# One list that orders the loads, the q/k part and the first 21 steps of a fused attention and two-expert kernel

## The chip, the cores and the metric

The kernel runs on one core of a Trainium2 chip. The metric is the device time in microseconds of one execution; before the change the median of three runs is 1145.67 us.

## The reference

In short: the input tokens are 6016 rows of 256 channels. Attention runs over channels: q and k are normalised over the tokens, a 256 x 256 score matrix is formed, and a softmax over it mixes the channels of v. Two pairs of dense layers follow, each 256 to 2048 to 256, the first with a rational activation, the second with h * relu6(h + 3) / 6.

```python
qn = q / (np.linalg.norm(q, axis=1, keepdims=True) + 1e-06)
kn = k / (np.linalg.norm(k, axis=1, keepdims=True) + 1e-06)
s = kn.transpose(0, 2, 1) @ qn / tau
a = softmax(s)                    # rows of 256
x = (v @ a).reshape(6016, 256)
h = x @ w_in                      # float64 weights
g = (a0 + a1*h + a2*h*h + a3*h**3) / (1 + |b0|*|h| + |b1|*h*h + 1e-6)
x = g @ w_out
h = x @ w_in2
out = (h * clip(h + 3, 0, 6) / 6) @ w_out2
```

## The kernel before

**The front part.** q and k come in 14 chunks (QK_CHUNKS: 1, 2, ten of 4, 3 and 1 rows per partition). For each chunk ScalarE squares both tiles (L240), VectorE adds the squares into two accumulators (L242), and TensorE multiplies k against q (`products`, L250). When the accumulators are folded (L227), eight small matmuls sum them over the partitions (L281, L282), a chain of tiny VectorE and ScalarE instructions makes the inverse norms, a matmul with a diagonal matrix spreads the norms of q over the partitions (L304), ScalarE copies that row (L310), and the softmax follows (L319 to L327). The 256 x 256 result is then multiplied into w_in, in column groups W0a, W0b, W1, W2, W3 (L339), so that v goes straight into the first layer. ScalarE evicts the high half of each product (L349), VectorE the low half (L351); in the list these are E0ah0, E0al0 and so on.

**Weights.** The weights are float64 in memory. Each of the four matrices is loaded in four groups of 1 MB and made into a pair of tiles, high and low, by `conv`: piece s (ScalarE, L154), b (ScalarE, L156), j (VectorE, L160), h (ScalarE, L167) and the low half on VectorE (l) or POOL (p) (L171). `wi1:2b` is piece b of group 2 of the first w_in. w_in of the first expert needs only s, b and j.

**The steps.** v is cut into blocks of 384 and then eleven times 512 tokens. A step s handles two of the sixteen 128-row tiles of the hidden layer: M1 is the first layer of expert 1 (12 matmuls), then U1, P1 (ScalarE) and DS, P2, P3 (VectorE) read its PSUM tile h, and AB, LN, EX (ScalarE), HI, N2, DD (VectorE) and LO (VectorE) or LOP (POOL) make the high and low halves of the activation. M3 is the second layer for step s - 2. Ten steps behind, expert 2 runs: M2 (first layer), C1 (ScalarE), C2 (VectorE), H2 (ScalarE), L2 (VectorE) or L2P (POOL), M4. Yh and Yl split the output of expert 1 at the end of a block, Vh and Vl split v. In a full step TensorE does 48 matmuls of 512 columns.

**What sets the order.** TensorE, VectorE, ScalarE and POOL run in program order: `chain` ties each instruction to the one before on its engine. From the norm on, the program order up to step 21 is the list FILL, written out by hand; after it, and for what the list leaves out, the string ORDER repeats step by step. Loads go through SP's queue in the order in which they are called: q and k first (L233), then wi1, wo1, wi2 (L124, L127), with v and wo2 called where the list reaches certain steps. Buffers come from pools by tag (BUFS): three each of U, P, hi, lo, which hold the chunks of q and k first, two of B, C and st. A load into a buffer waits until its last readers are done. Instructions of two engines that read the same PSUM tile are put one after the other in program order. `shares` marks a VectorE instruction that reads two SBUF operands, and `behind` makes a POOL instruction wait for the last marked one.

Of the kernel before, what the change touches and what calls it, by code (L numbers as in the profile page):

```python
# [61 lines left out]
def attention_rational_relu6_kernel(ctx: ExitStack, tc, q, k, vT, tau, w_in, w_out, ca, cb, w_in2, w_out2, outT):  # L62
# [44 lines left out]

# [144 lines left out]

    for i in range(LAST + 1):
        load_chunk(i)
        if i == LAST:
            for n in (512, 256):
                for a in (acc_k, acc_q):
                    fold(a, n)
        squares(i)
        if i <= NORM_AT:  # L260
            products(i)
    nc.sync.dma_start(out=TAU, in_=tau.partition_broadcast(128))
    load_w("wi1", 0)
    nc.sync.dma_start(out=col[:, 4:6], in_=cb.partition_broadcast(128))
    nc.sync.dma_start(out=col[:, 0:4], in_=ca.partition_broadcast(128))
    load_w("wi1", 1)
    load_v(0)
    load_w("wi1", 2)
    load_w("wi1", 3)
    for name in ("wo1", "wi2"):  # L270
        for g in range(4):
            load_w(name, g)
# [3 lines left out]
    nc.vector.reciprocal(out=rt, in_=TAU)
    s2k, s2q = tails
    for i in range(4):
        a, t = ((acc_k, s2k), (acc_q, s2q))[i // 2]
        h = slice((i % 2) * 128, (i % 2) * 128 + 128)  # L280
        nc.tensor.matmul(ssp[:, 0, i:i + 1], a[:, h], ones[:, 0:1], start=True, stop=False)  # L281
        nc.tensor.matmul(ssp[:, 0, i:i + 1], t[:, h], ones[:, 0:1], start=False, stop=True)  # L282
# [19 lines left out]
    nc.vector.tensor_scalar(out=inv[:, 0:2], in0=inv[:, 0:2], scalar1=rt, scalar2=-1.0, op0=ALU.mult, op1=ALU.mult)
    products(LAST - 1)
    nc.tensor.matmul(ssp[:, 1, 0:256], ones, diag, start=True, stop=True)  # L304
    products(LAST)
    for p in "sbj":
        conv("wi1", 1, p)
    split_v(0, "h")
    split_v(0, "l")
    nc.scalar.activation(out=qb, in_=ssp[:, 1, 0:256], func=AF.Copy)  # L310
    conv("wi1", 2, "s")
# [324 lines left out]
```

## Time and profile before

| | |
|---|---|
| median of the runs | 1145.67 us (1145.56 to 1145.82) |
| span of the profiled execution | 1141.5 us |
| its own time | not recorded apart; with the median it leaves 4.2 us around the span |
| TensorE busy | 1100.4 us (96%), 4870 matmuls |
| VectorE busy | 1009.6 us (88%) |
| ScalarE busy | 819.8 us (72%) |
| POOL busy | 251.6 us (22%) |
| loaded and stored | 42.2 MB, nearly all loads in the first 83 us |

The span runs from the first instruction to the last. Busy shares are averages over stages with different limits: q/k products first, then the ramp of expert 1 with the weight pieces, then the steps of both experts. A row of the trace counts matmuls as the hardware issues them: a chunk of four rows has 16 in the q/k part.

### The profile page before, as it was taken

To read this page: it belongs to the slowest core of one execution; us is meant where nothing else is said; L and a number is where in the kernel's file an instruction comes from. 1 tells how busy PE (TensorE), PEld (TensorE's weight loads), DVE (VectorE), ACT (ScalarE), POOL (GpSimd) and SP (SyncE) were. 2 spreads that over 40 slices of the span, in tenths; PEclk is the share of its full clock that TensorE was granted. 3 is DMA by queue.
4 is the path that set the end of the run, shared out by engine and by line. 5 is a ranking of instruction groups with operands and counts; after the bars stand their busy time and mean duration, and the time that the engine had idled before them with its cause. 6 is when DMAs were issued, how large, how long until landed. Compare 5 with 4: busy or idle time off the path is not lost.

```text
span 1141.5 us, 12312 instructions
## 1 busy us (share of the span) xinstructions
PE 1100.4 (96%) x4870; PEld 914.1 (80%) x4870; DVE 1009.6 (88%) x872; ACT 819.8 (72%) x802; POOL 251.6 (22%) x115
## 2 busy tenths in 40 slices
PE   8986689999999999999999999999999999999998
PEld 7756578877888888888888888888888888888887
DVE  6689999988999999998998998998998999999954
ACT  6798986776776777777677676786776776776643
POOL 0013335222221222212212222122122221221200
PEclk9998899999999999999999999999999999999999
DMA  9980000000010010010010010010010010000000
GB/s 358 369 327 1 19 1 1 15 19 1 1 37 1 1 38 1 1 37 1 1 37 1 1 38 1 1 37 1 1 37 1 1 37 1 1 19 1 1 19 18
DMA packets 17464, 42.20 MB, mean 37 GB/s; under 512 B 1536, under 2 KB 2560, under 8 KB 17408
## 3 DMA queue, kind: packets, MB, share of 16 engines
q1 hardware_dynamic: 17408, 41.43, 9.9%
q8 instruction: 38, 0.62, 0.2%
q14 instruction: 18, 0.15, 0.0%
HBM read 35.26 MB, written 6.16 MB: 36 GB/s over the span
## 4 chain that ended last, share of the span: by engine, by line
PE 86%; DVE 6%; ACT 4%; issue 2%; DMA 1%; POOL 0%; SPq 0%; POOLq 0%; DVEq 0%; ACTq 0%
PE h L374 41%; PE y L379 21%; PE o L379 20%; PE y L250 3%; DVE B L421 1%; ACT P L406 1%; DVE P L430 1%; DVE P L416 1%; ACT U L411 1%; DVE hi L544 1%; DVE P L556 1%; DMA lo<-in_q_dram 1%; DVE B L550 1%; ACT U L434 0%; DVE q L160 0%
## 5 line engine op out<-in xcount | busy, mean ns | idle before, releaser
L485 POOL TENSOR_TENSOR lo<-C,hi 128x1024 fp32r<-128x1024 f32 (+1 forms) x82 | 195.4, 2383 | 680.5 <-DVE lo L561 649.6
L411 ACT ACTIVATE U<-h,col 128x1024 f32<-128x1024 f32 (+1 forms) x96 | 105.7, 1101 | 180.2 <-PE h L374 179.6
L374 PE MATMUL h<-vh,w 128*128 128x512 f32 (+1 forms) x768 | 194.7, 397 | 20.0 <-DVE P L430 18.8
L379 PE MATMUL y<-hi,wo 128*128 128x512 f32 (+1 forms) x800 | 198.7, 385 | 0.4 <-DVE hi L544 0.4
L374 PEld LDWEIGHTS h<-vh,w 128*128 128x128 f32 x768 | 147.9, 195 | 52.7 <-issue 21.5
L374 PE MATMUL h<-yh,wi 128*128 128x512 f32 (+1 forms) x768 | 187.1, 385 | 3.0 <-DVE C L474 1.8
L379 PE MATMUL o<-hi,wo 128*128 128x512 f32 (+1 forms) x736 | 182.6, 384 | 0.0
L421 DVE SCALAR_TENSOR_TENSOR B<-U,aB,h 128x1024 f32<-128x1024 f32 (+1 forms) x96 | 120.6, 1256 | 61.8 <-ACT P L406 61.6
L379 PEld LDWEIGHTS y<-hi,wo 128*128 128x128 f32 x800 | 149.3, 188 | 29.2 <-DVE hi L544 0.7
L374 PEld LDWEIGHTS h<-yh,wi 128*128 128x128 f32 x768 | 143.2, 188 | 32.3 <-DVE C L474 3.2
L379 PEld LDWEIGHTS o<-hi,wo 128*128 128x128 f32 x736 | 137.6, 188 | 26.6
L469 ACT ACTIVATE C<-h,imm 128x1024 f32<-128x1024 f32 (+1 forms) x96 | 105.1, 1095 | 62.6 <-PE h L374 60.0
L474 DVE SCALAR_TENSOR_TENSOR C<-C,h 128x1024 f32<-128x1024 f32 (+1 forms) x96 | 114.0, 1187 | 16.1 <-ACT C L469 16.1
L544 DVE SCALAR_TENSOR_TENSOR hi<-P,col,U 128x1024 fp32r<-128x1024 f32 (+1 forms) x96 | 125.3, 1306 | 1.0 <-ACT U L438 0.9
L430 DVE SCALAR_TENSOR_TENSOR P<-P,col,h 128x1024 f32<-128x1024 f32 (+1 forms) x96 | 120.7, 1257 | 3.9 <-ACT U L411 1.2
L556 DVE SCALAR_TENSOR_TENSOR P<-P,col,B 128x1024 f32<-128x1024 f32 (+1 forms) x96 | 121.0, 1261 | 2.7
L406 ACT ACTIVATE P<-h,col 128x1024 f32<-128x1024 f32 (+1 forms) x96 | 113.3, 1181 | 6.9 <-PE h L374 5.1
L550 DVE SCALAR_TENSOR_TENSOR B<-B,hi 128x1024 f32<-128x1024 f32 (+1 forms) x96 | 115.8, 1207 | 2.7
L416 DVE TENSOR_TENSOR P<-P,h 128x1024 f32<-128x1024 f32 (+1 forms) x96 | 114.5, 1193 | 3.4 <-ACT U L411 1.9
L480 ACT ACTIVATE hi<-C 128x1024 fp32r<-128x1024 f32 (+1 forms) x96 | 99.6, 1037 | 23.8 <-DVE C L474 21.8
L379 PE MATMUL y<-lo,wo 128*128 128x512 f32 (+1 forms) x400 | 108.3, 388 | 7.6 <-POOL lo L561 7.6
L434 ACT ACTIVATE U<-B,imm 128x1024 f32<-128x1024 f32 (+1 forms) x96 | 108.9, 1134 | 2.7
(101 smaller groups left out, 1296.6 us busy)
## 6 DMA issues: line engine op xcount, KB each, us to landing
raw_wi<-in_moe_w_in_dram SPq DMA_DIRECT2D x8, 1024.0 KB, 13.4
raw_wo<-in_moe_w_out_dram SPq DMA_DIRECT2D x8, 1024.0 KB, 15.1
vo<-in_v_dram SPq DMA_DIRECT2D x11, 512.0 KB, 3.7
out_dram<-vo SPq DMA_DIRECT2D x10, 512.0 KB, 2.8
...
```

Source lines behind the costliest of these rows:

```text
L374: nc.tensor.matmul(h[j], w_in_at(name, a, c, f + j), x[b][:, c, :], start=(i == 0), stop=(i == 5))
L379: nc.tensor.matmul(y[d], w_out_at(name, a, 2 * pr + j, d), g[b][j], start=(pr == 0 and i == 0), stop=(pr == 7 and i == 5))
L406: nc.scalar.activation(out=halves(c["P"], T), in_=c["h"], func=AF.Identity, scale=A3, bias=A2)
L411: nc.scalar.activation(out=halves(c["U"], T), in_=c["h"], func=AF.Abs, scale=B1)
L416: nc.vector.tensor_tensor(out=p, in0=p, in1=c["h"], op=ALU.mult)
L421: nc.vector.scalar_tensor_tensor(out=halves(c["B"], T), in0=halves(c["U"], T), scalar=aB0, in1=c["h"], op0=ALU.add, op1=ALU.mult)
L430: nc.vector.scalar_tensor_tensor(out=p, in0=p, scalar=A1, in1=c["h"], op0=ALU.add, op1=ALU.mult)
L474: nc.vector.scalar_tensor_tensor(out=x, in0=x, scalar=6.0, in1=h, op0=ALU.min, op1=ALU.mult)
L485: i2 = e.tensor_tensor(out=x, in0=y, in1=z.bitcast(F32), op=ALU.subtract)
L544: shares(nc.vector.scalar_tensor_tensor(out=c["Hi"][:, fa], in0=P[:, fa], scalar=A0, in1=U[:, fa], op0=ALU.add, op1=ALU.mult))
L550: shares(nc.vector.scalar_tensor_tensor(out=B[:, fa], in0=B[:, fa], scalar=ONE_EPS, in1=c["Hi"][:, fa].bitcast(F32), op0=ALU.add, op1=ALU. ...
L556: shares(nc.vector.scalar_tensor_tensor(out=P[:, fa], in0=P[:, fa], scalar=A0, in1=B[:, fa], op0=ALU.add, op1=ALU.subtract))
```

## The change

The loads, the q/k part and the norm are cut into pieces with names of their own and put into FILL, which now begins the program. `lq3` loads chunk 3 of q, `lwi12` loads group 2 of the first w_in, `lst`, `lsa`, `lsb` the scalars, `lv1` block 1 of v; `sq3` squares, `aq3` adds, `x3` multiplies, `fk512` folds, `nT` to `nC` are the norm, `zm0` to `zr0` the softmax. ORDER is unchanged.

- Loads: q13 and k9 come early; the first weight load (wo1:0) comes between q10 and q11, more between and behind the last chunks; wo2 and v are called from the list.
- Weight pieces of wo1:0, wi1:0, wi1:2, wo1:1, wo1:2, wi2:2 stand between the pieces of the q/k part, the norm and the softmax.
- The norm matmuls (nM) come after product x11; before, after x10.
- The order of all steps to 21 is another, also the order in which U1, P1, DS, P2, P3 read a PSUM tile. LOP stands 18 times (14 before), LO 2 (6), L2P 8 (6), L2 3 (5); weight low halves are 8 on POOL and 4 on VectorE in both, but other ones.
- The tiles of the low halves (Lo, L2, vl, yl) are asked for where they are written, not with the high halves.
- LOP now waits for the last marked VectorE instruction (`behind`).

```diff
 FILL = (
...
+    "lq0 lk1 lk0 lk2 sq0 aq0 lq1 sq1 lq2 lq13 sq2 lk3 x0 sk0 x1 lq3 lq5 ak0 aq1 sq3 sk1 lk4 x2 lq4 aq2 ak1 lk9 sk2 lk5 lst x3 ak2 "
+    "sq4 x4 lq6 lq7 lsb aq3 sk3 aq4 ak3 x5 sq5 lk6 lq8 sk5 aq5 sk4 sq7 x6 sq6 ak4 ak5 lk8 aq6 lk7 sk6 ak6 sk8 lk10 x7 sk7 sq8 lq9 "
+    "aq7 ak7 lq10 ak8 sq9 aq8 sk9 x8 ak9 sk10 sq10 lwo10 lq11 lk11 aq9 lk13 lk12 lq12 aq10 wo1:0b x9 lwi10 wo1:0s ak10 wo1:0j sk11 "
+    "sq11 sq12 ak11 wo1:0h aq11 sk12 x10 aq12 sq13 ak12 fk512 x11 sk13 nB lwo11 fq512 fk256 wi1:0s wi1:0b wo1:1b nT wo1:1s fq256 "
+    "lwi12 lwo12 nM wi1:0j n0 wi1:2b wo1:0p n1 x12 lwi22 n2 wi1:2s wo1:2s nD x13 nC wo1:2b wi1:2j zm0 ze0 zm1 wi2:2s ze1 lwi11 zt0 "
+    "zc0 wi1:1s wi1:1b wi2:2b zt1 wo1:1j zc1 lv0 zr0 lwi13 wi1:1j W0a wo1:2j E0ah0 W0b Vh lwo13 wi2:2j E0ah1 E0al0 wi1:3s W1 wi1:3b "
+    "E0bh1 Vl E0al1 M1@0 E0bh0 E1h1 lsa wo1:2h E1h0 U1@0 lwi20 P1@0 E0bl1 wi1:3j E0bl0 M1@1 E1l1 wo1:1h lwo20 E1l0 U1@1 P2@0 W3 "
+    "DS@0 P1@1 wo1:1p P3@0 P2@1 DS@1 P3@1 AB@0 M1@2 LN@0 wo1:2p E3h1 EX@0 AB@1 E3l1 lv1 M1@3 E3h0 HI@1 E3l0 W2 N2@1 LN@1 EX@1 HI@2 "
+    "P1@2 U1@2 DD@1 N2@2 wo1:3s wi2:2h E2h0 LOP@1 P2@2 E2h1 DS@2 P3@2 AB@2 DD@2 U1@3 E2l1 LN@2 LOP@2 E2l0 M1@4 EX@2 DS@3 HI@3 "
+    "wo1:3b N2@3 wo1:3j P1@3 AB@3 P1@4 DD@3 U1@4 P2@3 LN@3 M3@2 DS@4 wi2:2p LOP@3 P2@4 wo2:0s lwi21 M3@3 P3@3 AB@4 M1@5 P3@4 EX@3 "
+    "LN@4 M1@6 EX@4 HI@4 U1@5 HI@5 wi2:0b N2@4 P1@5 N2@5 wo2:0b wi2:1s DD@4 P2@5 DS@5 LOP@4 M3@4 U1@6 P3@5 DD@5 wo2:0j AB@5 P1@6 "
+    "M1@7 P2@6 Vh@7 LN@5 LOP@5 DS@6 P3@6 EX@5 M3@5 HI@6 Vl@7 AB@6 LN@6 N2@6 EX@6 M1@8 HI@7 wo2:0h M3@6 lwo23 wo1:3h lwo22 P1@7 DD@6 "
+    "lwo21 N2@7 U1@7 wi2:0s LO@6 DD@7 P2@7 U1@8 M3@7 wo2:0p P1@8 wo2:2b DS@7 DS@8 P3@7 P2@8 AB@7 LOP@7 wo1:3p LN@7 M1@9 EX@7 AB@8 "
+    "LN@8 wo2:1s P3@8 M1@10 EX@8 HI@8 wi2:0j U1@9 N2@8 P1@9 lwi23 wi2:0h wi2:1b HI@9 DD@8 wo2:1b N2@9 LOP@8 M3@8 P1@10 U1@10 M3@9 "
+    "P2@9 DS@9 Yh@9 AB@9 LN@9 DD@9 P3@9 P2@10 Yl@9 wi2:0p EX@9 lv2 LOP@9 P3@10 DS@10 M2@10 wo2:2s M1@11 C1@10 HI@10 wi2:1j M3@10 "
+    "N2@10 wo2:2j AB@10 LN@10 DD@10 EX@10 U1@11 P1@11 C2@10 LOP@10 P2@11 DS@11 P3@11 H2@10 L2P@10 wi2:1h AB@11 HI@11 M3@11 M2@11 "
+    "C1@11 wo2:2h M1@12 wi2:1l C2@11 LN@11 H2@11 U1@12 wo2:2l M2@12 P1@12 C1@12 N2@11 DD@11 M4@11 DS@12 EX@11 AB@12 C2@12 L2P@11 "
+    "P2@12 LN@12 P3@12 LOP@11 EX@12 H2@12 M4@12 M2@13 HI@12 N2@12 C1@13 M1@13 wo2:1j U1@13 DD@12 M3@12 C2@13 P1@13 wi2:3b wo2:1h "
+    "P2@13 LOP@12 DS@13 L2P@12 M2@14 M3@13 P3@13 HI@13 AB@13 LN@13 wo2:1l wi2:3s N2@13 C1@14 M1@14 H2@13 wi2:3j M4@13 DD@13 U1@14 "
+    "C2@14 P1@14 L2P@13 P2@14 LOP@13 wi2:3h DS@14 P3@14 M4@14 M2@15 EX@13 HI@14 H2@14 N2@14 M1@15 M3@14 AB@14 wi2:3l DD@14 LN@14 "
+    "EX@14 C1@15 L2P@14 U1@15 C2@15 P1@15 Vh@15 P2@15 DS@15 LOP@14 AB@15 P3@15 LN@15 HI@15 M2@16 M4@15 M3@15 Vl@15 M1@16 N2@15 "
+    "EX@15 C1@16 wo2:3s HI@16 C2@16 U1@16 DD@15 N2@16 LO@15 P1@16 M2@17 DD@16 H2@15 P2@16 LOP@16 wo2:3b DS@16 P3@16 L2@15 M3@16 "
...
+    "AB@20 L2@19 HI@20 H2@20 N2@20 DD@20 LOP@20 P1@21 U1@21 C1@21 LN@20 DS@21 C2@21 M4@20 EX@20 P2@21 L2P@20 AB@21"
 )
...
+    def square(x, i):
+        s2 = sq[x, i] = wtile("B" if x == "k" else "st")[:, 0:QK_CHUNKS[i] * 256]
+        nc.scalar.activation(out=s2, in_=chunks[x, i], func=AF.Square)
...
             @add
             def HI():
                 first = pend.pop(a)
                 U, B, P = c["pend"] = first["U"], first["B"], first["P"]
-                c["Hi"], c["Lo"] = wtile("hi", F32R), wtile("lo", F32R)
+                c["Hi"] = wtile("hi", F32R)
...
             def lo(e):
                 U, B, P = c["pend"]
+                c["Lo"] = wtile("lo", F32R)
+                hl1[a] = [halves(c[t], Ta) for t in ("Hi", "Lo")]
                 i = e.tensor_tensor(out=c["Lo"][:, fa], in0=P[:, fa], in1=U[:, fa], op=ALU.mult)
-                if e is nc.vector:
-                    shares(i)
+                (shares if e is nc.vector else behind)(i)
...
-            if n == "M1" and int(at) % 8 == 4:
-                load_v(int(at) // 8 + 1)
+        elif n[0] == "l":
+            if n[1] in "kq":
+                load_chunk(n[1], int(n[2:]))
...
             w1_matmuls(n[1:])
-            if n != "W0a":
-                load_w("wo2", int(n[1]))
```

## Rows read from the trace of the kernel before

**Rows 1.** Busy by stretch: length, PE, PEld, DVE, ACT, POOL, clock, DMA, GB/s.
```profile
50.00:59.88 9.88, 7.45 (x30) 4.91 (x29) 6.82 (x13) 8.28 (x12) 0.00 (x0) 1.00 1.05 391
59.88:144.21 84.33, 59.10 (x246) 49.47 (x244) 76.88 (x80) 78.12 (x89) 24.52 (x11) 0.88 0.28 104
144.21:162.64 18.43, 15.46 (x73) 12.80 (x73) 18.16 (x17) 15.80 (x16) 9.01 (x4) 1.00 0.00 0
162.64:210.16 47.52, 46.69 (x228) 40.92 (x228) 44.67 (x41) 33.92 (x36) 16.44 (x6) 1.00 0.00 1
210.16:255.78 45.62, 44.90 (x204) 37.88 (x205) 41.56 (x34) 32.81 (x32) 11.19 (x6) 1.00 0.06 21
255.78:272.73 16.95, 14.43 (x61) 11.03 (x60) 12.84 (x12) 11.61 (x11) 4.58 (x2) 1.00 0.00 0
272.73:1128.00 855.27, 855.27 (x3775) 708.43 (x3774) 768.29 (x632) 601.27 (x564) 183.16 (x76) 1.00 0.04 12
```

**Rows 2.** Timeline of TensorE: start, us, line, operation, count [idle before, releaser].
```profile
37.48 3.62 PE L250 MATMUL y<-lo,hi 128*128 128x256 f32 x16
...
40.93 0.28 PE L281 MATMUL o<-ones,accs 128*128 128x1 f32 x2
...
48.76 0.59 PE L304 MATMUL o<-yl,ones 128*128 128x256 f32 x2
...
59.88 1.96 PE L374 MATMUL h<-vh,w 128*128 128x384 f32 x8
...
162.64 1.67 PE L374 MATMUL h<-yh,wi 128*128 128x384 f32 x8 [1.05 <-DVE C L474]
```

**Rows 3.** Waits of TensorE and VectorE, 60 to 165 us: total us, times, longest.
```profile
PE h L374 <- DVE P L430: 16.2, 5, 7.3
...
PE y L379 <- POOL lo L561: 7.4, 3, 4.2
...
DVE w L351 <- ACT w L349: 3.6, 3, 1.8
```

**Rows 4.** Busy time by stretch, two stretches of the q/k stage.
```profile
10.00:20.00 10.00, 10.00 (x48) 8.79 (x48) 9.00 (x9) 8.23 (x9) 0.00 (x0) 1.00 1.02 413
...
30.00:40.00 10.00, 10.00 (x48) 8.81 (x47) 9.56 (x12) 7.16 (x9) 0.00 (x0) 1.00 0.87 316
```

**Rows 5.** Timeline of ScalarE (two rows), then of VectorE (two rows), q/k stage.
```profile
9.72 1.06 ACT L240 ACTIVATE st<-lo 128x1024 f32<-128x1024 f32 x1 [0.80 <-DMA lo<-in_q_dram]
...
12.29 1.06 ACT L240 ACTIVATE st<-P 128x1024 f32<-128x1024 f32 x1 [0.22 <-DMA P<-in_q_dram]
...
21.04 1.23 DVE L242 TENSOR_TENSOR accs<-accs,st 128x1024 f32<-128x1024 f32 x1
...
37.75 1.96 DVE L227 TENSOR_TENSOR accs<-accs 128x512 f32<-128x512 f32 x4
```

**Rows 6.** Groups by line: count, busy us, mean ns, idle before.
```profile
L156 ACT ACTIVATE raw_wo<-raw_wo,imm 128x1024 int32<-128x1024 uint16 x8 | 10.0, 1247 | 0.0
```

**Rows 7.** Timeline of VectorE: an evict, a weight piece, the instruction after it.
```profile
67.96 0.75 DVE L351 SCALAR_TENSOR_TENSOR w<-o,small,w 128x512 fp32r<-128x512 f32 x1
...
91.26 1.22 DVE L160 SCALAR_TENSOR_TENSOR q<-q,raw_wo 128x1024 int32<-128x1024 int32 x1
...
92.39 1.01 DVE L556 SCALAR_TENSOR_TENSOR P<-P,col,B 128x768 f32<-128x768 f32 x1
```

**Rows 8.** Timeline of VectorE (two rows of line 544), then of POOL.
```profile
137.49 2.92 DVE L544 SCALAR_TENSOR_TENSOR hi<-P,col,U 128x1024 fp32r<-128x1024 f32 x1
...
143.78 1.27 DVE L544 SCALAR_TENSOR_TENSOR hi<-P,col,U 128x1024 fp32r<-128x1024 f32 x1
...
137.48 1.84 POOL L561 TENSOR_TENSOR lo<-P,U 128x768 fp32r<-128x768 f32 x1
```

**Rows 9.** Timeline of VectorE, then of TensorE, where the list ends.
```profile
266.02 1.28 DVE L421 SCALAR_TENSOR_TENSOR B<-U,aB,h 128x1024 f32<-128x1024 f32 x1 [2.78 <-ACT P L406]
...
269.89 2.09 PE L374 MATMUL h<-vh,w 128*128 128x512 f32 x8 [1.23 <-DVE P L430]
```

More of the change, by code (lines that the diff above doesn't have):

```diff
@@ L251, in products @@
                                  qt[:, r * 256:(r + 1) * 256], start=(first[i] + r == 0), stop=(first[i] + r == PER - 1))
[L253 to L272, printed above, removed]
-    rt = small[:, 0:1]
[L276 to L282, printed above, removed]
@@ L283, in attention_rational_relu6_kernel @@
-    for p in "sbj":
-        conv("wi1", 0, p)
-    products(NORM_AT + 1)
+        parts_done.append(i)
+    rt = small[:, 0:1]
     aB0 = const.tile([128, 1], F32, name="aB0")
-    nc.scalar.activation(out=aB0, in_=B0, func=AF.Abs)
     ss, ln, y0, iy, nrm, inv = (small[:, 4 * j:4 * j + 4] for j in range(1, 7))
-    nc.vector.tensor_scalar(out=ss, in0=ssp[:, 0, 0:4], scalar1=1e-30, scalar2=None, op0=ALU.max)
-    nc.scalar.activation(out=ln, in_=ss, func=AF.Ln)
-    nc.scalar.activation(out=y0, in_=ln, func=AF.Exp, scale=0.5)
@@ L302, in attention_rational_relu6_kernel @@
[L302 to L311, printed above, removed]
     nmax, sm, rs = small[:, 28:30], small[:, 30:32], small[:, 2:4]
-    ep = ptile("h1")
@@ L316, in attention_rational_relu6_kernel @@
-    eT = halves(wtile("hi"), 256)
     half = [slice(c * 256, (c + 1) * 256) for c in range(2)]
-    for c, h in enumerate(half):
-        nc.vector.scalar_tensor_tensor(out=sc[:, h], in0=sp[:, c, 0:256], scalar=inv[:, c:c + 1], in1=qb, op0=ALU.mult, op1=ALU.mult)
-        nc.vector.tensor_reduce(out=nmax[:, c:c + 1], in_=sc[:, h], axis=AX.X, op=ALU.min)
-    for c, h in enumerate(half):
-        nc.scalar.activation(out=sc[:, h], in_=sc[:, h], func=AF.Exp, scale=-1.0, bias=nmax[:, c:c + 1], accum_out=sm[:, c:c + 1])
-        for d in range(2):
-            nc.tensor.transpose(ep[:, c, d * 128:(d + 1) * 128], sc[:, c * 256 + d * 128:c * 256 + (d + 1) * 128], ident)
-        nc.vector.tensor_copy(out=eT[:, :, c * 128:(c + 1) * 128], in_=ep[:, c, 0:256].rearrange("p (d t) -> p d t", d=2))
@@ L326, in attention_rational_relu6_kernel, with norm @@
-    nc.vector.tensor_scalar(out=rs, in0=sm, scalar1=1e-9, scalar2=None, op0=ALU.add)
-    nc.vector.reciprocal(out=rs, in_=rs)
+    late = {}
+    def norm(part):
+        if part == "T":
+            nc.vector.reciprocal(out=rt, in_=TAU)
+        elif part == "B":
+            nc.scalar.activation(out=aB0, in_=B0, func=AF.Abs)
+        elif part == "M":
+            for i in range(4):
+                x = "kq"[i // 2]
+                h = slice((i % 2) * 128, (i % 2) * 128 + 128)
+                nc.tensor.matmul(ssp[:, 0, i:i + 1], acc[x][:, h], ones[:, 0:1], start=True, stop=False)
+                nc.tensor.matmul(ssp[:, 0, i:i + 1], sq[x, LAST][:, h], ones[:, 0:1], start=False, stop=True)
+        elif part == "0":
+            nc.vector.tensor_scalar(out=ss, in0=ssp[:, 0, 0:4], scalar1=1e-30, scalar2=None, op0=ALU.max)
+        elif part == "1":
+            nc.scalar.activation(out=ln, in_=ss, func=AF.Ln)
+            nc.scalar.activation(out=y0, in_=ln, func=AF.Exp, scale=0.5)
+        elif part == "2":
+            nc.vector.reciprocal(out=iy, in_=y0)
+            nc.vector.tensor_tensor(out=iy, in0=iy, in1=ss, op=ALU.mult)
+            nc.vector.tensor_tensor(out=nrm, in0=y0, in1=iy, op=ALU.add)
+            nc.vector.tensor_scalar(out=nrm, in0=nrm, scalar1=0.5, scalar2=1e-6, op0=ALU.mult, op1=ALU.add)
+            nc.vector.reciprocal(out=inv, in_=nrm)
+            late["yl"], late["yh"] = wtile("yl"), wtile("yh")
+            diag = late["diag"] = late["yl"][:, 0:256]
+            late["sc"], late["qb"] = late["yl"][:, 256:768], late["yh"][:, 0:256]
+            for c in range(2):
+                nc.vector.tensor_scalar(out=diag[:, c * 128:(c + 1) * 128], in0=ident, scalar1=inv[:, 2 + c:3 + c], scalar2=None, op0=ALU.mult)
+            nc.vector.tensor_scalar(out=inv[:, 0:2], in0=inv[:, 0:2], scalar1=rt, scalar2=-1.0, op0=ALU.mult, op1=ALU.mult)
+        elif part == "D":
+            nc.tensor.matmul(ssp[:, 1, 0:256], ones, late["diag"], start=True, stop=True)
+        else:
+            nc.scalar.activation(out=late["qb"], in_=ssp[:, 1, 0:256], func=AF.Copy)
@@ new lines, in softmax @@
+    def softmax(part, c):
+        h, sc = half[c], late["sc"]
+        if part == "m":
+            nc.vector.scalar_tensor_tensor(out=sc[:, h], in0=sp[:, c, 0:256], scalar=inv[:, c:c + 1], in1=late["qb"], op0=ALU.mult, op1=ALU.mult)
+            nc.vector.tensor_reduce(out=nmax[:, c:c + 1], in_=sc[:, h], axis=AX.X, op=ALU.min)
+        elif part == "e":
+            nc.scalar.activation(out=sc[:, h], in_=sc[:, h], func=AF.Exp, scale=-1.0, bias=nmax[:, c:c + 1], accum_out=sm[:, c:c + 1])
+        elif part == "t":
+            if not ep:
+                ep.append(ptile("h1"))
+            for d in range(2):
+                nc.tensor.transpose(ep[0][:, c, d * 128:(d + 1) * 128], sc[:, c * 256 + d * 128:c * 256 + (d + 1) * 128], ident)
+        elif part == "c":
+            if len(ep) == 1:
+                ep.append(halves(wtile("hi"), 256))
+            nc.vector.tensor_copy(out=ep[1][:, :, c * 128:(c + 1) * 128], in_=ep[0][:, c, 0:256].rearrange("p (d t) -> p d t", d=2))
+        else:
+            nc.vector.tensor_scalar(out=rs, in0=sm, scalar1=1e-9, scalar2=None, op0=ALU.add)
+            nc.vector.reciprocal(out=rs, in_=rs)
@@ L504, in Yh @@
                     c["y"] = yp.pop(y)[:, :, 0:T]
-                    y_hl[y] = [halves(wtile(t, F32R), T) for t in ("yh", "yl")]
+                    y_hl[y] = [halves(wtile("yh", F32R), T)]
                     nc.scalar.activation(out=y_hl[y][0], in_=c["y"], func=AF.Copy)
@@ L586, in fill @@
             do(n, int(at))
-            if n == "M1" and int(at) % 8 == 4:
-                load_v(int(at) // 8 + 1)
+        elif n[0] == "l":
+            if n[1] in "kq":
+                load_chunk(n[1], int(n[2:]))
+            elif n[1] == "v":
+                load_v(int(n[2:]))
+            elif n[1] == "w":
+                load_w(n[1:4], int(n[4]))
+            else:
+                load_small(n[2])
+        elif n[0] == "s":
+            square(n[1], int(n[2:]))
+        elif n[0] == "a":
+            add_square(n[1], int(n[2:]))
+        elif n[0] == "f":
+            fold(n[1], int(n[2:]))
+        elif n[0] == "x":
+            products(int(n[1:]))
+        elif n[0] == "n":
+            norm(n[1])
+        elif n[0] == "z":
+            softmax(n[1], int(n[2]))
         elif ":" in n:
```

61 lines of the change are left out of this document (28 added, 33 removed), and 27 rows, old and new, of the table FILL.

## The prediction

> **What bounds the kernel now.** I read the busy table by stretch first. From 272.73 us to 1128 us TensorE is busy 855.27 of 855.27 us at the full clock, so nothing that the list of the first steps does can shorten that part; it can only start it sooner [rows 1]. The time that can move lies before. Between the first expert's first matmul group (M1@0, 59.88 us) and M2@12 (162.64 us), 102.76 us pass [rows 2]; TensorE is busy 59.10 + 15.46 = 74.6 us of them, VectorE 76.88 + 18.16 = 95.0 us, ScalarE 78.12 + 15.80 = 93.9 us, and the granted clock is 0.88 in the first of the two stretches, a mix of 2.4 and 1.2 GHz that TensorE's gaps bring [rows 1]. The waits say who is waited for: TensorE stands 16.2 us for a VectorE reader of the PSUM tile and 7.4 us for the low halves from POOL [rows 3]. So VectorE bounds this stretch, with ScalarE just behind. After 162.64 us TensorE takes over: 46.69 busy of 47.52, 44.90 of 45.62, then 14.43 of 16.95 where the list ends [rows 1]. In all 4.1 us are left to win there.
>
> The span is 1141.5 us and the median of the runs 1145.67, so 4.2 us lie around the span; I take the profiled execution for one like the timed ones and carry the 4.2 unchanged. With the last stretches fixed, the new time is the old one less what M2@12 comes earlier, corrected for TensorE work moved across that point.
>
> **The change, part by part.**
>
> *Loads.* The same bytes go through the same queue. Before, the transfers ran at 413 GB/s with q and k alone, and fell to 316 where the queue waited for buffers [rows 4]. The new list has tile 13 of q and tile 9 of k early, so they hold a buffer each; q5 then waits on SP until product x1 has freed its buffer, and k4, q4 queue behind it. At 0.41 MB per us from q2's landing (its square starts at 9.72 us [rows 5]), the remaining 11.5 MB of q, k and wo1:0 take until about 38 us, and the products ask for a chunk only every 3.45 us [rows 2]. So I cost the q/k supply at nothing; if that cover is gone, each us that a chunk is late is a us for all that follows. Of the weights, wi1:2 lands by the same rate at about 45.5 us and wo1:2 at 48 us, just before ScalarE's list wants them. The loads of wo2 and v move too, but their users come tens of us later: nothing.
>
> *Squares and sums.* ScalarE now does sq1 and sq2 before sk0, and sq3 before sk1. The squares of q2 and q3 could not start before 9.72 and 12.29 us [rows 5], so VectorE gets its sums some 5 us later than now and then works through them at 1.23 us and a small gap apiece. It ended the folds at 39.7 us [rows 5]; I get about 45 us, with one weight piece (wo1:0j) inside. The norm matmuls are moved behind x11, whose end is at about 44.4 us (40.93 us now [rows 2] plus one chunk of 3.45). So this costs 0 to 1 us.
>
> *Norm and softmax.* Diag's matmul comes after the same TensorE work as before (all products but the last), so its 48.76 us [rows 2] is the earliest. But weight pieces now stand in the chain on in-order engines: wi1:2b before Ln, wi1:2s and wo1:2s before the copy of the norm row, wo1:2b and wi2:2s before the two Exp, wo1:1j between the two copies of the transposes. At 1.25 us for a b piece [rows 6], no more for an s, and 1.13 for a j piece [rows 7] this is 7.4 us if none lies in a gap, and 0 if all do. The chain leaves gaps (VectorE was busy 6.82 and ScalarE 8.28 of the last 9.88 us before M1@0 [rows 1]) and waits of its own between engines; I let rather more than half of the pieces fall there and take 3 us. M1@0 then stands at 62.9 us instead of 59.88, bounds 59.9 to 68 with the 1 us above.
>
> *VectorE's work between M1@0 and M2@12.* I counted both lists. Only before: LO@5, LO@10, N2@11, four j pieces (wo1:1, wo1:2, wi2:2, wo2:1) and four l pieces (wo1:1, wo1:2, wo2:0, wo2:1). Only after: LO@6, E1l0, wi1:3j and l pieces of wi2:1 and wo2:2. Back to back an instruction of 1024 columns occupies 1.13 us from start to start, a 512-column evict at most 0.75 [rows 7]; LO@5 and LO@6 cancel. So 10 x 1.13 less (0.75 + 3 x 1.13) = 7.2 us go. Three of the j pieces went into the gaps before M1@0, three l pieces to POOL; the rest is postponed. ScalarE loses twelve instructions and gains three, of about a us each, so it does not take VectorE's place.
>
> M2@12 then comes at 62.9 + 102.76 - 7.2 = 158.5 us, 4.1 us earlier. The new list has M1@12 ahead of that point (twelve matmuls of 512 columns, 12 x 855.27/3775 = 2.7 us [rows 1]) where the old one had M4@11 (384 columns, three quarters of it), so TensorE is 0.7 us further: 4.8 us.
>
> *VectorE's idle time in that stretch*, 102.76 - 95.04 = 7.7 us [rows 1]. Of it 3.6 us are waits of the low-half evicts for the high-half evicts [rows 3]. The new list puts j pieces between them; I take 1.5 us back, bounds 0 and 3.6.
>
> *POOL's low halves wait for the shared port.* Each LOP now waits for the last VectorE instruction marked as sharing. Before, one LOP started at 137.48 us together with HI, which took 2.92 us instead of 1.27 [rows 8]. I take 1 us back, bounds -2 and +2. Behind a waiting LOP queue POOL's weight pieces and L2P, and M3 of the next step waits for it: up to 1.2 us each, hidden while M3 runs late in its step. More pieces go to POOL: LOP 14 to 18, L2P 6 to 8. The Trainium skill, "SBUF — State Buffer", section "SBUF: two separate sides", says that VectorE and GpSimd lock one port pair for a whole instruction, whichever starts first. The 2.92 us agree with it; by it each moved piece could hold VectorE up for as long as it saves, which is the third rival.
>
> *Tiles asked for later* (Lo, L2, vl, yl): HI and H2 no longer wait for a buffer of the low half. No idle time in front of HI shows such a wait: nothing.
>
> *After M2@12.* The list reorders readers of PSUM tiles. Its end is better: U1, P1 and DS of step 21 are in it, where now DS waited 2.78 us for P1 and TensorE 1.23 us behind it [rows 9]. I give 1.5 us for it. Against it, from M2@12 to M2@17 the lists, counted in the same way, hold 44.1 us for VectorE and 42.6 for TensorE, where they held 43.9 and 45.3, because weight pieces were postponed into it; TensorE will idle 1.5 us. Net nothing, bounds -4 and +4.1.
>
> Sum: 4.8 + 1.5 + 1 = 7.3 us: 1145.67 - 7.3 = 1138.4 us.
>
> **The rivals.**
> 1. *Much better.* All 7.7 us of idle time go, the weight pieces fall wholly into gaps and the 4.1 us after M2@12 go: 3 more from the start, 5 more from the idle time, 4 from the end, 19 in all, 1126 us. For it: one list now orders loads and engines together. Against: the chain M1, U1, P1, DS of one step stays.
> 2. *It does not do what it says.* The pieces pulled ahead of M1@0 delay it by about what they save (by 7 us rather than 3), and the evict waits stay: 4.8 + 1 - 4 = 2 us, 1144 us, hardly to be told from no change. For it: ScalarE has only 1.6 us of gaps in the 9.88 us before M1@0 [rows 1].
> 3. *The port.* VectorE held up by POOL. The price is 1.65 us a hit [rows 8]; POOL runs some 15 pieces before M2@12. Five more hits would use up the 7.3 us; eight more give 13.2 - 7.3 = 5.9 us slower, 1151.6 us. Against: the new wait is there to avoid just that.
> 4. *The front starves, slower.* Weights and q/k share one in-order queue and in-order engines: wi1:2b stands before Ln, wo1:2s before the norm row. At 413 GB/s wo1:2 lands at 48 us; at 316 [rows 4] the 15.8 MB from q2 on take 50 us rather than 38.5, it lands at 60 us, W0 starts at 66 and M1@0 at 73 us: 10 us later than I take, 3 us slower, 1148.5 us. It decides from M1@0 after 70 us. Against: SP's waits in the new order are all released before the queue runs dry, by my count.
>
> **How the numbers follow.** Forecast 0.58, rival 1 0.13, rival 2 0.12, rival 3 0.06, rival 4 0.11. The measurement tells 0.2%, 2.3 us, from nothing. Faster: 0.56 of the forecast, 0.13, and 0.03 of rival 2: 0.72. Same: 0.02 + 0.07 = 0.09. Slower: rivals 3 and 4 and 0.02 of rival 2: 0.19. The forecast's own range is 1133 to 1143 us; with the bounds of the start and of the idle time, and half of each side's rivals, 1129 to 1148 us.
>
> **What will show it.** M1@0 between 62 and 64 us (the start); the VectorE adds ending at about 45 us; M2@12 at 154 to 159 us; VectorE over 95% busy between the two with 7 us less work; no HI of 2.9 us; the wait of the low-half evicts shorter. Wrong if M1@0 comes after 70 us, if TensorE waits for weights or for q/k loads beyond 10 us, or if TensorE still has gaps of a us and more after 175 us.

## The result, and the profile after

The changed kernel takes 1129.01 us (median; 1128.56 to 1129.92), the kernel before 1145.74 us beside it: a ratio of 0.9856 (0.9842 to 0.987). The forecast was 1138.4 us: the right side, but a gain of 7.3 us where 16.7 came, and its range reached to 1129.0.

A second profile of the kernel before was taken 

> The kernel before, once more, to see how its span stands to its time. Time 1145.6 to 1145.9. If the profiled execution of before was a quick one, this span is 1143.5 to 1144 and 1.8 us lie around it, as in the changed kernel; if 4.2 us really lie around it, the span is 1141.5.

It ran in 1145.79 us with a span of 1143.5, so 2.3 us lie around the span and not 4.2: the execution profiled first was a quick one. M1@0 came at 61.76 us and M2@12 at 164.64. The execution of [rows 2] had reached M1@0 1.9 us sooner, so the differences below are against the second profile:

```profile
61.76:164.64 102.88, 75.14 (x318) 62.80 (x316) 95.01 (x96) 93.86 (x104) 33.49 (x15) 0.90 0.21 78
164.64:274.72 110.08, 105.99 (x492) 89.88 (x493) 99.11 (x85) 78.37 (x78) 32.22 (x13) 1.00 0.03 9
```

With M2@22 for the first group behind the list (274.72 us there, 257.70 after), the 16.7 us of the span are: M1@0 4.6 later (66.31), M1@0 to M2@12 16.1 shorter (102.88 to 86.76), M2@12 to M2@22 5.5 shorter (110.08 to 104.63), the rest 0.3 longer.

Busy time by stretch after, answering to [rows 1] (columns as there):

```profile
66.31:134.68 68.37, 54.88 (x247) 46.62 (x245) 66.68 (x72) 65.54 (x76) 25.99 (x13) 0.91 0.30 107
134.68:153.07 18.39, 17.87 (x72) 14.96 (x73) 18.08 (x17) 15.58 (x16) 7.59 (x4) 0.87 0.00 0
153.07:196.27 43.20, 43.10 (x217) 38.88 (x216) 42.43 (x38) 35.79 (x37) 16.91 (x8) 1.00 0.00 1
196.27:238.66 42.39, 41.68 (x193) 35.21 (x192) 36.48 (x33) 32.35 (x33) 13.81 (x6) 1.00 0.07 22
238.66:257.70 19.04, 19.04 (x85) 15.77 (x84) 18.00 (x15) 13.91 (x14) 7.20 (x3) 1.00 0.00 0
257.70:1113.00 855.30, 855.30 (x3775) 708.47 (x3774) 767.81 (x632) 601.23 (x564) 182.99 (x76) 1.00 0.04 12
```

Up to M2@12 VectorE is busy 66.68 + 18.08 = 84.76 of 86.76 us: 10.3 us less work than before (95.01) and 2.0 us idle where there were 7.9. The granted clock has no part in it: 0.90 before, 0.91 and 0.87 in the two stretches after. From M2@12 to M2@22 TensorE has 0.8 us of gaps where it had 4.1. The long last stretch is what it was. The waits of TensorE (four rows) and VectorE (four rows) from 66 to 153 us, beside [rows 3]:

```profile
PE h L359 <- DVE P L415: 8.7, 4, 3.5
PE y L364 <- POOL lo L549: 2.1, 2, 1.7
PE h L359 <- ACT yh L492: 2.0, 1, 2.0
PE h L359 <- DVE w L336: 1.2, 1, 1.2
...
DVE w L336 <- ACT w L334: 1.1, 2, 0.8
DVE hi L531 <- ACT U L423: 0.5, 2, 0.2
DVE P L401 <- issue: 0.3, 1, 0.3
DVE P L401 <- ACT P L391: 0.3, 1, 0.3
```

TensorE's wait for P3, the last reader of the tile, is half of what it was, and so is the longest (7.3 to 3.5 us). VectorE's waits for the tiles of P1 and U1 were these before (60 to 165 us):

```profile
DVE B L421 <- ACT P L406: 1.7, 2, 0.9
DVE P L416 <- ACT P L406: 1.3, 2, 1.1
DVE P L416 <- ACT U L411: 0.6, 2, 0.3
```

The front became slower. A product with the wait before it, the norm matmuls, product x12, diag's matmul and M1@0 on TensorE (beside [rows 2]); then two stretches of the q/k stage (beside [rows 4]); then SP's queue:

```profile
30.88 3.69 PE L242 MATMUL y<-P,U 128*128 128x256 f32 x16 [1.06 <-DMA U<-in_k_dram]
...
48.23 0.28 PE L262 MATMUL o<-ones,accs 128*128 128x1 f32 x2
...
49.93 2.84 PE L242 MATMUL y<-lo,hi 128*128 128x256 f32 x12
...
53.32 0.70 PE L282 MATMUL o<-yl,ones 128*128 128x256 f32 x2 [0.55 <-DVE yl L279]
...
66.31 0.91 PE L359 MATMUL h<-vh,w 128*128 128x384 f32 x2
```

```profile
10.00:20.00 10.00, 10.00 (x41) 8.48 (x40) 5.88 (x7) 4.80 (x7) 0.00 (x0) 1.00 0.77 290
20.00:30.00 10.00, 9.82 (x46) 8.27 (x44) 8.61 (x8) 6.59 (x8) 0.00 (x0) 1.00 0.95 363
```

```profile
4.48 7.65 SPq L224 DMA_DIRECT2D P<-in_q_dram  x2
```

The loads of q3 and q5, one row here, hold SP for 7.65 us, of which 6.6 are its longest wait for a product; the transfers fell to 290 GB/s where they had run at 413. Product x12 of the second profile before:

```profile
46.45 2.75 PE L250 MATMUL y<-lo,hi 128*128 128x256 f32 x12
```

So the products themselves, as many as before, are 3.5 us late, which is most of the 4.6 us at M1@0.

### The profile page after: what moved, and what is told of

Same layout as the page of the kernel before. It is cut to its first block, busy times and chain, and to the rows that moved or that the text cites. A ratio compares the mean times of both kernels' runs of the same rounds, so it can differ in the third digit from the quotient of the medians.

```text
span 1126.8 us, 12304 instructions
## 1 busy us (share of the span) xinstructions
PE 1100.6 (98%) x4870; PEld 916.1 (81%) x4870; DVE 998.3 (89%) x866; ACT 817.2 (73%) x802; POOL 259.6 (23%) x121
## 4 chain that ended last, share of the span: by engine, by line
PE 85%; DVE 1%; ACT 1%; POOL 1%; issue 0%; POOLq 0%; ACTq 0%; DVEq 0%
PE h L359 43%; PE y L364 21%; PE o L364 21%; ACT U L396 0%; DVE P L401 0%; POOL lo L549 0%; DVE B L406 0%; POOL wi L166 0%; ACT B L410 0%; POOL lo L471 0%; ACT P L391 0%; DVE P L542 0%; ACT U L419 0%; DVE B L536 0%; DVE hi L531 0%
## 5 line engine op out<-in xcount | busy, mean ns | idle before, releaser
L471 POOL TENSOR_TENSOR lo<-C,hi 128x1024 fp32r<-128x1024 f32 (+1 forms) x84 | 199.0, 2369 | 662.3 <-DVE lo L549 637.9
L359 PE MATMUL h<-vh,w 128*128 128x512 f32 (+1 forms) x768 | 190.2, 390 | 10.6 <-DVE P L415 9.4
L359 PEld LDWEIGHTS h<-vh,w 128*128 128x128 f32 x768 | 144.2, 190 | 41.7 <-issue 8.6
L531 DVE SCALAR_TENSOR_TENSOR hi<-P,col,U 128x1024 fp32r<-128x1024 f32 (+1 forms) x96 | 122.1, 1272 | 3.3 <-issue 2.1
## 6 DMA issues: line engine op xcount, KB each, us to landing
raw_wi<-in_moe_w_in_dram SPq DMA_DIRECT2D x8, 1024.0 KB, 13.8
```

The lines of the kernel that those rows point to most:

```text
L359: nc.tensor.matmul(h[j], w_in_at(name, a, c, f + j), x[b][:, c, :], start=(i == 0), stop=(i == 5))
L471: i2 = e.tensor_tensor(out=x, in0=y, in1=z.bitcast(F32), op=ALU.subtract)
L531: shares(nc.vector.scalar_tensor_tensor(out=c["Hi"][:, fa], in0=P[:, fa], scalar=A0, in1=U[:, fa], op0=ALU.add, op1=ALU.mult))
```

## The experiments

Each was timed in three rounds. Edits are to the changed kernel's list, unless said otherwise.

**Code without the list.** A_old_list: changed code, the whole old order.

> The changed kernel's code with the old order of everything (loads, q/k part, norm, softmax, steps): only the code edits remain, the wait of LOP for the last marked VectorE instruction and the later requests of the low halves' buffers. Theory (the order of the list is what counts): 1143.5 to 1146, a gain of 0 to 2 us, HI of 2.9 us gone. Rival 1 (the code edits carry much of the gain): 1141 or less.

1146.44 us, ratio 1.0003 (0.9992 to 1.0015). With the old list the edits outside it are worth nothing that the runs can tell; the order is all of the gain. Two single code edits agree. H_early_buffers asks for Lo, L2, vl and yl with the high halves again; D_no_lop_wait drops LOP's new wait:

```diff
-                (shares if e is nc.vector else behind)(i)
+                if e is nc.vector:
+                    shares(i)
```

> New list, but the buffers of the low halves (Lo, L2, vl, yl) are asked for together with those of the high halves, as before the change. Theory (no wait hung on it, as with the old order of the list, where the edits of the code without the list came to 1146.44 against 1145.8): 1128 to 1130 us. Rival (with five low halves more on POOL the buffers stay taken longer, and HI now waits for them): 1131 us or more, with waits in front of HI.

> The changed kernel with LOP not waiting for the marked VectorE instruction. Theory: 1129.5 to 1132, some HI or N2 of over 1.6 us come back, each costing up to 1.6 us of VectorE. Rival 1: 1134 or more. If the wait itself costs more than it saves: below 1128.

H took 1130.35 us (1128.69 to 1130.44), D 1130.1 us (1128.53 to 1131.54): no difference that these runs can tell. The long HI and N2 that D was to bring back did not come.

**The new front alone.** C_new_front_old_steps: new list to M1@0, then the old order of what is left.

> The new list up to M1@0 and then the old order of the steps, without the weight pieces that the new front has done. Theory (the order of the steps carries most; the front saves 7 us of VectorE work behind M1@0 and gives 6.4 back by the later M1@0): 1140 to 1145. Rival 2 (the front with its weight pieces in the gaps is the gain): 1134 or less. M1@0 at 66 us either way.

1149.23 us, ratio 1.0026 (1.0016 to 1.0036): slower, and both theories missed. M1@0 came at 67.85 us, and M1@0 to M2@12 still took 100.57 us:

```profile
67.85:168.42 100.57, 74.21 (x318) 62.20 (x316) 91.40 (x93) 86.50 (x96) 28.93 (x14) 0.88 0.19 70
```

VectorE has 3.6 us less to do than before, but 9.2 us idle. The new front costs 6 us and gives back 2; some 20 us of gain, from here to the changed kernel, are in the order of the steps together with its split over POOL and VectorE.

**The readers of the PSUM tile.** F_reader_order puts them in one order at their own places (52 tokens), for instance:

```diff
- U1@5 ... P1@5 ... P2@5 DS@5 ... P3@5
+ U1@5 ... P1@5 ... DS@5 P2@5 ... P3@5
```

> New list, but the readers of each PSUM tile (U1, P1, DS, P2, P3) put back into one fixed order U1, P1, DS, P2, P3 at the same five places of the list (52 tokens change place). Theory (the order of the readers is what takes VectorE's idle time between M1@0 and M2@12 from 9.2 to 2.0 us): 3 to 6 us slower, 1132 to 1135 us, and idle time of VectorE back at 5 to 8 us in that stretch. Rival (the interleaving of the steps does it, the order within a tile is worth nothing): 1128 to 1130 us.

1133.38 us, 4.4 slower, as the theory had it, though the idle time came back to 4.3 us only and not to 5 to 8; M1@0 to M2@12:

```profile
66.40:156.56 90.16, 73.66 (x318) 61.48 (x317) 85.89 (x88) 81.30 (x90) 33.61 (x16) 0.91 0.22 80
```

Of the 3.4 us more, 2.3 are VectorE idle (4.3 for 2.0) and 1.1 work. The reverse, R_new_readers, the new reader order at the old list's places, gave no result, because its order deadlocks; so whether this order is a gain by itself stays open.

**POOL or VectorE.** G_old_split gives the low halves the old list's engines back (18 tokens), K_old_steps_new_split does the reverse in C's list (edit of G, ten of its tokens):

```diff
- wo1:1p ... wo1:2p ... LOP@5 ... LO@6 ... wo2:0p ... LOP@10 ... wi2:1l ... L2P@11 ... LOP@11 ... L2P@13 ...
+ wo1:1l ... wo1:2l ... LO@5 ... LOP@6 ... wo2:0l ... LO@10 ... wi2:1p ... L2@11 ... LO@11 ... L2@13 ...
```

> New list, but each low half and weight piece goes back to the engine that it had in the old list (18 tokens change engine between POOL and VectorE; places stay). By the durations in the trace this gives VectorE about 2.3 us more work before M2@12 and 3 to 5 us more in all of the first 21 steps. Theory (VectorE bounds the stretch, so its work counts in full, and the rest of the gain is order): 2 to 5 us slower, 1131 to 1134 us. Rival (POOL's side decides, the moves to POOL are what the new order needs): over 8 us slower, 1137 us or more. Third (moves hidden): within 1 us of 1129.

> New front with the old order of the steps, as in C_new_front_old_steps (1149.23 us), but the low halves and weight pieces go to the engine (POOL or VectorE) that they have in the new list: 18 tokens change engine. Undoing the same 18 in the new list cost 14 us. Theory 1 (the split is a gain by itself): the 14 us come back here, about 1135 us. Theory 2 (the split only pays with the new order, which postpones weight pieces behind M2@12 where VectorE then has no room for low halves; before, VectorE was busy 99 of the 110 us behind M2@12 and TensorE stood only 4 us): 1143 to 1148 us, M1@0 to M2@12 some 2 to 4 us shorter than the 100.6 us of C.

G took 1142.82 us, 13.8 slower; K took 1156.91 us, ratio 1.0099 (1.0084 to 1.0114), 7.7 slower than C and outside both of its theories. So the split is no gain by itself: it fits its own order, and each list is hurt by the other's. In G the time goes with VectorE's work, as the theory had it, but there is more of it than was counted: M1@0 to M2@12 is 4.2 us longer (90.98) with 3.9 us more work (88.67), M2@12 to M2@22 9.4 us longer (114.02) with 8.5 us more (105.38). K shows another way (VectorE by shape, M1@0 to M2@12: count, busy us, mean ns; three operations without a PSUM operand, the three readers of PSUM, then one weight piece):

```profile
L544 DVE SCALAR_TENSOR_TENSOR P<-P,col,B 128x768 f32<-128x768 f32 x8 | 10.1, 1264 | 0.0
L533 DVE SCALAR_TENSOR_TENSOR hi<-P,col,U 128x768 fp32r<-128x768 f32 x8 | 9.9, 1239 | 0.0
L538 DVE SCALAR_TENSOR_TENSOR B<-B,hi 128x768 f32<-128x768 f32 x8 | 8.8, 1101 | 0.1
L408 DVE SCALAR_TENSOR_TENSOR B<-U,aB,h 128x768 f32<-128x768 f32 x8 | 8.1, 1008 | 1.4 <-ACT P L393 1.4
L417 DVE SCALAR_TENSOR_TENSOR P<-P,col,h 128x768 f32<-128x768 f32 x8 | 8.0, 1005 | 0.0
L403 DVE TENSOR_TENSOR P<-P,h 128x768 f32<-128x768 f32 x8 | 7.6, 949 | 1.3 <-ACT P L393 1.1 <-issue 0.2
L157 DVE SCALAR_TENSOR_TENSOR q<-q,raw_wo 128x1024 int32<-128x1024 int32 x4 | 6.5, 1622 | 0.0
```

The first three operations in the changed kernel, 66.31 to 134.68 us:

```profile
L531 DVE SCALAR_TENSOR_TENSOR hi<-P,col,U 128x768 fp32r<-128x768 f32 x8 | 8.3, 1037 | 0.5 <-ACT U L423 0.5
L542 DVE SCALAR_TENSOR_TENSOR P<-P,col,B 128x768 f32<-128x768 f32 x8 | 8.1, 1013 | 0.0
L536 DVE SCALAR_TENSOR_TENSOR B<-B,hi 128x768 f32<-128x768 f32 x8 | 7.5, 952 | 0.0
```

K has as many VectorE instructions there as C (93), but 97.4 us of work for 91.4. The readers of PSUM keep their length; what reads only SBUF is longer where POOL works beside it. In this stretch of K's trace nine VectorE instructions of 768 or 1024 columns with SBUF operands alone overlap one of POOL by 0.1 us or more, and six of them take over 1.5 us, up to 3.04; the 34 that overlap none take at most 1.28 us, and so do the 20 readers of PSUM that overlap one. In the changed kernel 37 readers of PSUM overlap POOL from M1@0 to M2@12, and of 40 SBUF-only ones a single one does (1.19 us).

**LOP's wait in lists that don't fit.** The same wait taken out of P (below), G, K and C.

> P_pieces_early (1139.29 us) without the wait of LOP for the shared port. In P_pieces_early LOP@8 stood 12.9 us behind a weight piece of VectorE (wo2:1j) and TensorE's M3@8 6.5 us behind LOP@8. Theory 1 (the loss of P was that wait: the wait is bound to the last VectorE instruction ahead of it in the list, so a moved weight piece drags POOL and TensorE with it): 1130 to 1133 us, what is left being two pieces of VectorE. Theory 2 (the loss is the place of the pieces on VectorE's and ScalarE's own queues, wi2:1b came late): 1136 us or more, M2@10 still later than 142 us.

> G_old_split (1142.82 us) without the wait of LOP. Theory 1 (part of the 14 us of G was the wait of LOP behind low halves that VectorE makes: POOL stood 57.8 us in seven such waits after 150 us): 1133 to 1138 us. Theory 2 (VectorE's own work behind M2@12, 105.4 us in place of 96.9, is the price): 1141 to 1144 us.

> K_old_steps_new_split (1156.91 us) without the wait of LOP. Theory 1 (the wait makes the mismatched list expensive): 1144 to 1150 us, below C (1149.23). Theory 2 (POOL's places in the old order are wrong for 18 other pieces, wait or not): 1154 us or more.

> C_new_front_old_steps (1149.23 us) without the wait of LOP. Theory 1 (as the wait cost nothing with the old list whole, A_old_list at 1146.44, and nothing with the new one): 1148 to 1150 us. Theory 2 (with the weight pieces pulled ahead the old steps' LOP stand behind other VectorE work): 1143 to 1147 us.

1139.39, 1146.21, 1156.34 and 1148.5 us, for 1139.29, 1142.82, 1156.91 and 1149.23 with it. It is not the wait that makes a wrong list dear; in G it even helps, by 3.4 us, which neither theory had.

**The place of weight pieces.** P_pieces_early:

```diff
- ... wi2:1b HI@9 DD@8 wo2:1b N2@9 LOP@8 M3@8 P1@10 U1@10 M3@9 P2@9 DS@9 ...
+ ... wi2:1b wi2:1j HI@9 DD@8 wo2:1b N2@9 wo2:1j LOP@8 M3@8 wo2:1h P1@10 U1@10 wi2:1h M3@9 wo2:1l P2@9 DS@9 wi2:1l ...
```

> New list, but the last three pieces of wi2:1 and of wo2:1 (j, h, l: four instructions of VectorE, two of ScalarE) come some two steps sooner, all ahead of M2@10; in the new list they stand behind it, those of wo2:1 behind M2@12. Theory (VectorE bounds TensorE up to M2@12 and not after it, so a postponed piece is a gain in full): M2@10 about 4.5 us later, M2@12 about 2.3 us later (the two pieces of wo2:1), and as nothing comes back behind it 1131 to 1132 us. Rival (the pieces lie in gaps, where they stand decides nothing): 1128 to 1130 us.

1139.29 us, 10.3 slower where 2.3 were expected. VectorE, POOL and TensorE there:

```profile
130.95 1.23 DVE L157 SCALAR_TENSOR_TENSOR q<-q,raw_wi 128x1024 int32<-128x1024 int32 x1 [4.28 <-ACT raw_wi L153]
132.09 1.28 DVE L533 SCALAR_TENSOR_TENSOR hi<-P,col,U 128x1024 fp32r<-128x1024 f32 x1
133.29 1.01 DVE L544 SCALAR_TENSOR_TENSOR P<-P,col,B 128x768 f32<-128x768 f32 x1
...
135.35 1.22 DVE L157 SCALAR_TENSOR_TENSOR q<-q,raw_wo 128x1024 int32<-128x1024 int32 x1
...
136.71 1.81 POOL L551 TENSOR_TENSOR lo<-P,U 128x768 fp32r<-128x768 f32 x1 [12.87 <-DVE q L157]
...
138.57 1.65 PE L366 MATMUL y<-lo,wo 128*128 128x384 f32 x4 [6.46 <-POOL lo L551]
```

The j piece of wi2:1 (130.95 us) stood at the head of VectorE's queue before ScalarE had its source, and held HI@9, DD@8, LOP@8 and M3@8 behind it; LOP@8 then waited for wo2:1j (135.35) as well. That second wait decides nothing, since P is as slow without it (PD_no_wait). M2@10 comes at 145.59 us, 10.9 later than in the changed kernel. The six moved pieces cost what waits behind them, not their length of about 1.2 us each.

**Behind M2@12.** L_old_tail has the new list to M2@12 and the old order from there; N_new_tail the old list to M2@12 and the new order and split from there.

> New list up to M2@12, then what is left in the order of the old list (with the new split over POOL and VectorE, and the readers of step 21 last). The span from M2@12 to the end was 978.9 us before and is 973.7 after. Theory (those 5.2 us are the order after M2@12: TensorE's gaps of 4.1 us there went): 4 to 6 us slower, 1133 to 1135 us, M2@12 within 0.5 us of 153.1. Rival (they are only TensorE work brought ahead of M2@12, and the granted clock): within 1.5 us of 1129.

> The other way round from L_old_tail: everything up to M2@12 in the old order (A_old_list, 1146.44 us, of which 978.9 us lie behind M2@12), and what is left from there in the order of the new list, with its split over POOL and VectorE. Theory (the 5.2 us behind M2@12 are the new order there, TensorE's gaps of 4.1 us going): 1141 to 1143 us, behind M2@12 974 to 976 us. Rival (the order behind M2@12 fits only what the new list leaves open before it): 1146 us or more.

L took 1145.82 us, but doesn't price the tail: the postponed weight pieces all fall in one place, and M2@12 to M2@13 alone takes 17.1 us (6.3 in the changed kernel). N took 1140.05 us, ratio 0.9953 (0.9939 to 0.9968), 6.4 better than A, with TensorE's gaps behind M2@12 down to 1.1 us:

```profile
166.45:276.00 109.55, 108.46 (x510) 92.96 (x509) 97.49 (x85) 81.45 (x82) 40.30 (x18) 1.00 0.03 9
```

The new order there, with its split, is a gain by itself, somewhat larger than its theory had it.

**The front.** E_pair_front loads and squares k and q in pairs up to chunk 10; E2_front and E3_front move the norm matmuls ahead of x11 as well and weight pieces behind the Ln.

```diff
- lq0 lk1 lk0 lk2 sq0 aq0 lq1 sq1 lq2 lq13 sq2 lk3 x0 ...
+ lk0 lq0 sk0 ak0 sq0 aq0 x0 lk1 lq1 sk1 ak1 sq1 aq1 x1 ...
```

> New list, but the front of it put into pairs up to chunk 10: the loads of k and q of a chunk together, then the two squares and sums, then the products, so that SP never stands behind product x1; the weight pieces in the front and all steps stay as in the new list. Theory (the blocked load queue and late squares are what put M1@0 at 66.3 us in place of 62.9 or less): the norm matmuls 3 to 5 us sooner than 48.2 us, M1@0 at 62 to 64 us, and the time 1125 to 1127 us. Rival (the start is set by the weight pieces between the engines' steps of the norm chain, not by the loads): M1@0 stays within 1 us of 66.3, 1128 to 1130 us.

> E_pair_front (1126.2 us) taken further: all loads of q and k in pairs up to chunk 13, the squares of the last chunks and the folds ahead of the weight pieces, the norm matmuls again ahead of product x11, and the weight pieces wi1:0, wo1:1, wi1:2 behind the Ln of the norm. Theory (M1@0 is set by the chain from the norm matmuls on, so each us by which they start sooner counts): norm matmuls at 42 us in place of 45.3, M1@0 at 62 to 63 us in place of 64.96, 1123.5 to 1125 us. Rival (the weight pieces then fill ScalarE between Ln and the copy of the norm row, and the chain gives the time back): M1@0 at 65 us or later, 1126 to 1128 us.

> E2_front mended: in E2_front the load of wo1:0 stood behind all of q and k and landed at 44.25 us, ScalarE waited 4.88 us for it with the Ln of the norm queued behind, and M1@0 came at 69.33 us. Here that load stands in the place that it has in E_pair_front (1126.2 us); the last squares, the folds and the norm matmuls stay ahead of the weight pieces, and three ScalarE pieces fewer stand ahead of the copy of the norm row. Theory (M1@0 follows the norm matmuls once no piece of the chain waits for a load): norm matmuls at 42 to 43.5 us, M1@0 at 62.5 to 64 us, 1123.5 to 1125.5 us. Rival (ScalarE is full from the last square on, so the pieces only change places): M1@0 at 65 to 66 us, 1126 to 1127 us.

E took 1126.2 us, ratio 0.9831 (0.9817 to 0.9846): faster than the kernel before, and by the medians 2.8 us faster than the changed one, though the two intervals still touch. Norm matmuls 45.33 us, M1@0 64.96: the time is the theory's, M1@0 is between theory and rival. It lies just below the executions of the new front in the other experiments (65.36 to 67.97 us). E2 and E3 had the norm matmuls at 43.28 us and M1@0 at 69.33 and 68.29: 1130.0 and 1131.68 us, slower than theory and rival of each. In E2 ScalarE waited for a load; in E3, behind the squares, for nothing of the kind, but five weight pieces stood between the copy of the norm row and the first Exp (ScalarE, end of the copy, the pieces, the Exp):

```profile
51.81 0.39 ACT L286 ACTIVATE yh<-o 128x256 f32<-128x256 f32 x1 [2.41 <-PE o L284]
52.10 1.22 ACT L153 ACTIVATE raw_wi<-raw_wi,imm 128x1024 int32<-128x1024 uint16 x1
53.21 1.10 ACT L151 ACTIVATE q<-raw_wi 128x1024 f32<-128x1024 f32 x1
54.22 2.16 ACT L151 ACTIVATE q<-raw_wo 128x1024 f32<-128x1024 f32 x2
56.25 1.24 ACT L153 ACTIVATE raw_wo<-raw_wo,imm 128x1024 int32<-128x1024 uint16 x1
57.36 0.53 ACT L294 ACTIVATE yl<-yl,small 128x256 f32<-128x256 f32 x1
```

The new list has one piece there. E, like it, does more of them earlier, between the squares.

## Why the prediction was right in sign and wrong in size

- **Loads cost nothing: wrong.** The wait of q5 for product x1 was foreseen, and priced at nothing because SP's queue was to refill before it runs dry. SP's wait was 6.6 us, TensorE then waited 1.06 us for a chunk of k, one of the signs of being wrong, and product x12 started 3.5 us late. E, without the wait, has x12 at 47.11 us and is 2.8 us faster, of which M1@0 shows 1.4; there diag's matmul waited 1.82 us for VectorE's part of the norm, so the products alone don't set the start. As E also puts the squares in pairs, it doesn't tell loads and squares apart.
- **Squares, sums, norm: M1@0 at 62.9 (bounds to 68), measured 66.31.** The folds ended at 47.9 us, not 45, and the norm matmuls came 3.8 us later than the 44.4 forecast. From there to M1@0 18.1 us passed, where the forecast had 18.5. So the miss lies ahead of the norm matmuls, and the sum for the weight pieces behind them came out, which no run tests by itself. Against the second profile the start cost 4.6 us, not 3.
- **VectorE's work, 7.2 us less: 10.3 measured.** Stretched instructions that went are 2.1 of the difference (three HI of 1024 columns 1821 ns before, 1281 after; three N2 of 1394, then 1216). The count went by places in the list and made it six instructions fewer; the trace has eight (96 and 88). Before, wo1:0j and E1l0, listed ahead of M1@0, ran beside and behind its start (61.00 and 63.09 us).
- **LOP's wait gives 1 us back: wrong cause.** No HI of 2.9 us is left, but D, without the wait, has none either; the new order is enough to remove it. In the old order with the wait it is gone too, up to M2@12 (A: HI of 1024 columns 1278 ns on the mean), and A is no faster for it.
- **VectorE's idle time, 1.5 us back (bounds 0 to 3.6): failed.** 5.9 went, 7.9 to 2.0. I bounded it by the wait of the low-half evicts alone, and took the waits for P1 and U1 as fixed by one step's chain. The new list has other work ready there: those waits fell from 3.6 us to 0.3, the evicts' from 3.6 to 1.1. F shows the order of the readers to be 2.3 us of it; C, with the new front and 9.2 us idle, shows that the rest is the order of the steps too, and not the split, as G idles 2.3 us only. Which moves of steps, I didn't separate.
- **After M2@12 net nothing (bounds -4 and +4.1): failed**, by 4.8 us, the largest miss. From 44.1 us of VectorE against 42.6 of TensorE in the counted lists I took a stall of 1.5 us. The trace has 42.43 busy of 43.20 for VectorE and 43.10 for TensorE: the count was too high for VectorE, which has less to do than TensorE there, and TensorE waits 0.1 us. Both engines are nearly full without one waiting for the other. Of the 5.5 us to M2@22, 3.3 are gaps and 0.7 is the work moved ahead; the rest is TensorE's busy time, shorter for as many matmuls (103.82 us for 105.99), which no run explains. N puts this gain, with the split, into the old list.
- **Tiles asked for later: right**, by H.

The misses are +4.8 (end), +4.4 (idle), +3.1 less the 1 put under LOP (work), -1.6 (start) and -0.3 (the rest of the span): 9.4 us in sum, which with the 7.3 make the 16.7. That the time lay at the very edge of the stated range is no merit of the sum: its terms for the idle time and the end both fell outside their own bounds, and the start missed the other way.

Rival 1 (1126 us) had the mechanism: idle time and end went, the start didn't. (Its sum takes 5 of the 6.2 us of idle time that the forecast leaves.) Rival 3, the port, isn't in this kernel but is in K, where VectorE needs 6 us more for as many instructions as in C. The Trainium skill, "SBUF — State Buffer", section "SBUF: two separate sides", says which VectorE instructions contend for the shared ports with one of GpSimd that reads SBUF: among others those with two SBUF inputs. The trace agrees: 1101 to 1622 ns for such instructions in K, and 949 to 1008 unchanged for those that read one operand from PSUM. Rival 4 needed M1@0 after 70 us.
